# Attention with memories and a gated feed-forward in one kernel: the scores of a steady batch in one tiled excursion, output additions and stores issued later

## The chip, the cores and the metric

The kernel runs on 1 core of one Trainium2 chip. The metric is the device time of one execution in microseconds; three executions of the kernel before took 689.68, 690.58 and 690.91 us, median 690.58.

## The reference

`B, H, S, D, M = 8, 8, 576, 64, 32`; the model width is `H*D = 512`, the inner width 2048.

```python
a = softmax(phi, axis=2)                      # over the 576 tokens, per memory
k_m, v_m = a^T k, a^T v                       # 32 memories of 64 per head
attn = softmax(q k_m^T / 8, axis=-1)          # over the 32 memories
x = (attn v_m) of all heads side by side      # 4608 x 512
h = x @ w_in                                  # 4608 x 2048
g = h * clip(h + 3, 0, 6) / 6
out = g @ w_out                               # 4608 x 512, float32
```

## The kernel before

`attn v_m` and `x @ w_in` are not made one after the other. For each batch the memories' values are multiplied into `w_in` first (`fold`, L424, result `both`), so that the first product of the feed-forward is `both` times the 256 probabilities of a token (8 heads by 32 memories). The kernel rounds each float32 operand to a high and a low part, so that a product of two float32 matrices is three matmuls.

Batches 0 and 1 and the rounding of the weights run in an opening whose order is written out by hand. Batches 2 to 7 are **steady**. Each has 32 half-steps, numbered i = 0 to 31: 16 for the first 256 tokens (`half` 0), 16 for the other 320 (`half` 1). A unit is two half-steps (k = 0, 1) and makes two blocks of 128 of the inner width for a half of the tokens. In a half-step TensorE runs `gemm1` (6 matmuls into a PSUM bank `ph`, L712), ScalarE `relu` (L718), VectorE `gate` (L731, for the last 64 tokens L735). Each unit then feeds a seven-product scheme for the second matrix product: VectorE adds blocks (L741) and GpSimd two more (L745, L746), ScalarE rounds them (L752), VectorE takes the low parts (L757), and TensorE runs `products` (L680): 9 matmuls with kept weights in odd half-steps, 3 with kept and 9 with streamed weights in even ones, for the unit three half-steps back. The streamed weights (`stream`, three blocks of 256 KB for each unit) come from HBM through SyncE's queue, two units ahead.

A **turn** is where a half ends. Its sums leave PSUM through ScalarE (`leave_first`, L785, L786, L791) and VectorE (`leave_second`, L794, L795), GpSimd adds twice (`leave_third`, L799, L800) and SyncE stores 512 KB (L802). The additions are issued at the end of half-step 2 or 18, ahead of the next unit's own GpSimd work. In batches 2, 4 and 6 the first half-steps also run a rest stage for the last 64 tokens of two earlier batches.

The attention of the next batch (N) is laid between these half-steps by the tables `STEADY` and `EVERY`: "16 sc.N.0" puts a word into half-step 16. C is the current batch, M the one after next. In a half-step with k = 0 the words come behind the previous unit's rounding, with k = 1 ahead of the unit's own rounding, in both ahead of `products`. The words that matter here are `mem` (the memories' moments, L319), `sc` (scores, L357), `ct` (VectorE transposes the scores out of PSUM, L373), `cm` and `cs` (maximum, centring), `fo`, `vh`, `vl` (fold and its rounding, `vl` is L444), `bt` (transpose back, L403), `sp` (a broadcast load `nmxb` of row maxima, L284), `q` and `pt` (loads), `fetch` (weights for `fold`, L213).

Scores and folds use matmuls on a part of TensorE's array, 64 rows by 32 columns, eight places at once. Such a group between matmuls on the whole array is called an excursion here. Scores of a half go to two PSUM banks of 512 columns:

```python
self.psc = [psc[:, g, : W[hf]] for g in range(NG)]
```

## Time and profile before

| | |
|---|---|
| median of 3 runs | 690.58 us (689.68 to 690.91) |
| the profiled execution's own time | 689.36 us |
| its span, first to last instruction | 687.5 us |
| TensorE matmul busy | 670.7 us (98%) |
| TensorE weight loads busy | 580.2 us (84%) |
| VectorE busy | 573.2 us (83%) |
| ScalarE busy | 399.5 us (58%) |
| GpSimd busy | 338.1 us (49%) |
| mean of one L741, L745, L746 (groups of the page) | 522, 967, 465 ns |
| granted TensorE clock, mean | 0.996 |
| DMA | 163.95 MB, mean 238 GB/s |

Busy times of an engine are the union of its instructions. Matmuls overlap in the engine's pipeline, so a busy TensorE may still wait: the gaps are seen better between weight loads, which follow each other closely when nothing is late. Names such as `acc<-w,rounded` say what an instruction writes and reads.

### The profile page before, as it was taken

To read this page: it belongs to the slowest core of one execution; us is meant where nothing else is said; L and a number is where in the kernel's file an instruction comes from. 1 tells how busy PE (TensorE), PEld (TensorE's weight loads), DVE (VectorE), ACT (ScalarE), POOL (GpSimd) and SP (SyncE) were. 2 spreads that over 40 slices of the span, in tenths; PEclk is the share of its full clock that TensorE was granted. 3 is DMA by queue.
4 is the path that set the end of the run, shared out by engine and by line. 5 is a ranking of instruction groups with operands and counts; after the bars stand their busy time and mean duration, and the time that the engine had idled before them with its cause. 6 is when DMAs were issued, how large, how long until landed. Compare 5 with 4: busy or idle time off the path is not lost.

```text
span 687.5 us, 15317 instructions
## 1 busy us (share of the span) xinstructions
PE 670.7 (98%) x5810; PEld 580.2 (84%) x5814; DVE 573.2 (83%) x1062; ACT 399.5 (58%) x819; POOL 338.1 (49%) x354
## 2 busy tenths in 40 slices
PE   8999999899999999999999999999999999999997
PEld 4446778688879998899889998889889998899997
DVE  4899997898996769986898769986899778988765
ACT  4686796464654556564565645665465655665553
POOL 2644430788564436544556336543448245555433
PEclk9999999999999999999999999999999999999999
DMA  9998592454957978869584696869585593836351
GB/s 354 419 348 312 171 349 83 157 154 168 326 207 250 334 269 280 282 217 338 173 296 161 212 342 185 294 226 340 210 285 211 170 323 123 267 129 219 122 186 47
DMA packets 66817, 163.95 MB, mean 238 GB/s; under 512 B 7096, under 2 KB 12216, under 8 KB 64696
## 3 DMA queue, kind: packets, MB, share of 16 engines
q1 hardware_dynamic: 66664, 162.91, 67.6%
q8 instruction: 46, 0.75, 0.4%
q14 instruction: 27, 0.22, 0.1%
q10 hardware_dynamic: 80, 0.07, 0.0%
HBM read 140.92 MB, written 22.03 MB: 237 GB/s over the span
## 4 chain that ended last, share of the span: by engine, by line
PE 77%; DVE 11%; DMA 5%; ACT 4%; issue 2%; POOL 1%; SPq 0%; ACTq 0%; DVEq 0%; POOLq 0%
PE acc L680 38%; PE ph L712 20%; PE acc L541 6%; PE pv L424 4%; PE ph L487 4%; PE pk L319 2%; DMA qh<-in_qt 2%; DVE tmp L172 1%; DVE tmp L180 1%; DMA w<-w_kept 1%; DMA pnat<-in_pn 1%; DMA stream<-kept 1%; DVE tmp L175 1%; DVE gf L503 1%; PE psc L357 1%
## 5 line engine op out<-in xcount | busy, mean ns | idle before, releaser
L680 PE MATMUL acc<-w,rounded 128*128 128x256 f32 x1536 | 213.5, 280 | 2.2 <-DVE rounded L757 1.9
L680 PEld LDWEIGHTS acc<-w,rounded 128*128 128x128 f32 x1536 | 192.4, 188 | 26.7 <-ACT gf L718 8.5
L745 POOL TENSOR_TENSOR gated<-gated 128x256 f32<-128x256 f32 x96 | 92.8, 967 | 222.3 <-DVE gated L731 203.9
L712 PE MATMUL ph<-probs,both 128*128 128x256 f32 (+1 forms) x1152 | 180.7, 292 | 0.0
L757 DVE TENSOR_TENSOR rounded<-gated,rounded 128x384 fp32r<-128x384 f32 x192 | 147.8, 771 | 29.7 <-ACT rounded L752 28.8
L752 ACT CAST rounded<-gated 128x384 fp32r<-128x384 f32 x192 | 108.5, 567 | 92.9 <-DVE gated L741 85.0
L712 PEld LDWEIGHTS ph<-probs,both 128*128 128x128 f32 x1152 | 157.6, 188 | 1.0 <-issue 0.8
L718 ACT ACTIVATE gf<-ph,three 128x256 f32<-128x256 f32 (+1 forms) x192 | 95.9, 500 | 67.1 <-PE ph L712 64.8
L680 PE MATMUL acc<-stream,rounded 128*128 128x256 f32 x864 | 116.0, 277 | 0.6 <-DMA stream<-kept 0.5
L731 DVE SCALAR_TENSOR_TENSOR gated<-gf,ph 128x256 f32<-128x256 f32 x192 | 79.1, 412 | 35.9 <-ACT gf L718 35.3
L680 PEld LDWEIGHTS acc<-stream,rounded 128*128 128x128 f32 x864 | 105.9, 188 | 2.2 <-DMA stream<-kept 1.9
L541 PE MATMUL acc<-w,ghi 128*128 128x512 f32 x224 | 59.2, 397 | 0.0
L487 PEld LDWEIGHTS ph<-probs,both 128*128 128x128 f32 x336 | 48.6, 193 | 11.8 <-DVE gf L503 8.1
L487 PE MATMUL ph<-probs,both 128*128 128x320 f32 (+1 forms) x336 | 52.2, 304 | 4.4 <-DVE gf L503 3.9
L741 DVE TENSOR_TENSOR gated<-gated 128x256 f32<-128x256 f32 x96 | 50.1, 522 | 1.6
L541 PEld LDWEIGHTS acc<-w,ghi 128*128 128x128 f32 x224 | 40.4, 189 | 12.8 <-issue 4.4
L435 ACT CAST both<-pv 128x512 fp32r<-128x512 f32 x62 | 36.0, 584 | 18.6 <-PE pv L424 13.4
L746 POOL TENSOR_TENSOR gated<-gated 128x128 f32<-128x128 f32 x96 | 44.7, 465 | 0.0
L444 DVE TENSOR_TENSOR both<-pv,both 128x512 fp32r<-128x512 f32 x62 | 41.9, 677 | 2.5 <-ACT both L435 2.1
L190 POOL TENSOR_TENSOR w<-tmp,raw 128x512 uint32<-128x512 uint32 x12 | 19.3, 1629 | 44.7 <-DVE tmp L180 25.1
L497 ACT ACTIVATE gf<-ph,three 128x576 f32<-128x576 f32 (+2 forms) x36 | 24.6, 687 | 21.0 <-PE ph L487 15.0
L424 PE MATMUL pv<-w,kvT 64*32 64x512 f32 (+1 forms) x528 | 35.1, 588 | 1.6 <-DVE pnat L302 0.9
(116 smaller groups left out, 852.6 us busy)
## 6 DMA issues: line engine op xcount, KB each, us to landing
stream<-kept SPq DMA_DIRECT2D x222, 256.0 KB, 4.7
w<-w_kept SPq DMA_DIRECT2D x40, 512.0 KB, 6.9
kvt<-in_kv SPq DMA_DIRECT2D x32, 516.0 KB, 7.1
raw<-in_w SPq DMA_DIRECT2D x16, 512.0 KB, 7.8
raw<-in_w SPq DMA_DIRECT2D x8, 1024.0 KB, 12.4
out_t<-o SPq DMA_DIRECT2D x16, 512.0 KB, 3.2
kept<-stage SPq DMA_DIRECT2D x24, 256.0 KB, 2.8
pnat<-in_pn SPq DMA_DIRECT2D x8, 576.0 KB, 5.3
```

The lines of the kernel that those rows point to most:

```text
L424: nc.tensor.matmul(to[j * M : (j + 1) * M, g, k], self.kvT[rows, g, j * M : (j + 1) * M], chunk[rows, k, j].bitcast(F32), start=True, stop ...
L487: nc.tensor.matmul(dst, w[:, g, fs], x[:, g * n : (g + 1) * n], start=(i == 0), stop=(i == len(seq) - 1),)
L541: nc.tensor.matmul(accs[self.b, self.rest, k].rearrange("p (x c) -> p x c", c=VC), left[:, t * P : (t + 1) * P], w, start=k in self.first ...
L680: nc.tensor.matmul(dst, left[l], right[r], start=begin and n == 0, stop=end and n == 2, skip_group_check=True)
L712: nc.tensor.matmul(h, w[:, g, fs], x[:, g * self.n : (g + 1) * self.n], start=(i == 0), stop=(i == len(seq) - 1))
L718: nc.scalar.activation(self.gf, self.h[k], AF.Relu, bias=three)
L731: nc.vector.scalar_tensor_tensor(dst, by_tile(self.gf), 6.0, by_tile(self.h[k]), ALU.min, ALU.mult)
L741: nc.vector.tensor_tensor(g[:, 5:7], g[:, 7:9], g[:, 0:2], ALU.add)
L745: nc.gpsimd.tensor_tensor(g[:, 2:4], g[:, 0::8], g[:, 1:8:6], ALU.subtract)
L746: nc.gpsimd.tensor_tensor(g[:, 4], g[:, 1], g[:, 7], ALU.add)
L752: nc.scalar.copy(self.parts[0][:, at], self.g[:, 1:8][:, at])
L757: nc.vector.tensor_tensor(low[:, at], self.g[:, 1:8][:, at], high[:, at].bitcast(F32), ALU.subtract)
```

## The change

Three things change. First, the words `sc.N.0`, `ct.N.0`, `sc.N.1`, `ct.N.1` of half-steps 16 to 20 become `sb.N` (`both_scores`), all scores of both halves in one excursion in half-step 16, and `cp.N.2`, `cp.N.0`, `cp.N.1` (`pair_turn`), their transposes. 256 tokens of each half share the two banks of 512 columns. The last 64 tokens go into free columns of two banks in use: columns 320 to 383 of the `ph` bank that the next `gemm1` writes, and the first 64 columns of the bank in which the running half keeps one block of sums. `sb` and `cp.N.2` are played ahead of the rounding. Second, where no rest stage follows, `leave_third` is issued one half-step later, behind the unit's own GpSimd work, and the store one half-step later still, behind the fetch of streamed weights. Third, many other words of the tables move.

```diff
-0 kv.N.2 / 1 kv.N.4 / 2 kv.N.3 / 4 kv.N.0 / 6 kv.N.1
+0 kv.N.0 kv.N.2 / 4 kv.N.4 kv.N.3 kv.N.1
...
-q.N.1 mem.N / 12 nr.N nk.N / 13 fetch.N.1.1 / 15 tp.N pt.M tk.N / 16 sc.N.0 ct.N.0 / 18 kv.M.0 / 19 sc.N.1 / 20 ct.N.1
+nk.N pt.M fetch.N.0.1 q.N.0 / 15 tp.N fetch.N.1.1 tk.N / 16 sb.N cp.N.2 / 17 cp.N.0 / 19 kv.M.0 cp.N.1 / 20 cm.N.0 /
...
@@ -245,7 +245,7 @@
             heads += [qh[:, j] for j in range(n)]
         loaded.setdefault(b, {})["q", hf] = heads
 
-    vw, probs = {}, {}
+    vw, probs, sums, turn = {}, {}, {}, [0]
 
     class Attention:
 
@@ -371,6 +371,39 @@
                     nc.vector.transpose(st[:, g], self.psc[g])
             else:
                 nc.vector.transpose(st, self.psc_whole)
+
+        def both_scores(self):
+            pa = self.psum("psc")
+            m1, spare = sums[self.b - 1, 0][1], ph[1 - turn[0]]
+            heads = loaded[self.b]
+            ends = [spare[:, W[1] : W[1] + REST], m1[:, :REST]]
+            self.pairs = [(hf, 0, W[0], [pa[:, g, hf * W[0] : (hf + 1) * W[0]] for g in range(NG)]) for hf in range(2)]
+            self.whole = [pa[:, :, hf * W[0] : (hf + 1) * W[0]] for hf in range(2)]
+            self.pairs.append((1, W[0], REST, ends))
+            for k, (hf, at, n, to) in enumerate(self.pairs):
+                for j in range(NJ):
+                    for g in range(NG):
+                        rows = slice(g * D, (g + 1) * D)
+                        nc.tensor.matmul(
+                            to[g][j * M : (j + 1) * M],
+                            self.kvT[rows, g, j * M : (j + 1) * M],
+                            heads["q", hf][j][rows, at : at + n],
+                            start=k == 0 or k == 2 and g == 0,
+                            stop=True,
+                            tile_position=(g * D, j * M),
+                            skip_group_check=True,
+                        )
+
+        def pair_turn(self, k):
+            hf, at, n, to = self.pairs[k]
+            if hf not in self.st:
+                self.st[hf] = sb.tile([P, NG * W[hf]], F32, name="st", tag="st", bufs=3)
+            st = self.st[hf].rearrange("p (g s) -> p g s", g=NG)
+            if at == 0:
+                nc.vector.transpose(st[:, :, :n], self.whole[hf])
+                return
+            for g in range(NG):
+                nc.vector.transpose(st[:, g, at : at + n], to[g])
 
         def by_token(self, hf):
             return self.st[hf].rearrange("p (n m) -> p n m", m=M)
@@ -704,6 +737,7 @@
             f = 2 * self.u + k
             self.h = self.h if k else {}
             h = self.h[k] = ph[k][:, : self.n]
+            turn[0] = k
             both = vw[self.b, f * P // VC]
             fs = slice(f * P % VC, f * P % VC + P)
             phi, plo = probs[self.b, self.half]
@@ -798,13 +832,14 @@
             o, x = self.o, self.x
             nc.gpsimd.tensor_tensor(o[:, 1:3], x[:, 0:2], x[:, 2:4], ALU.add)
             nc.gpsimd.tensor_tensor(o[:, 0::3], o[:, 0::3], x[:, 1:3], ALU.add)
+
+        def store(self):
+            o = self.o
             row = self.b * S + OFF[self.half]
             nc.sync.dma_start(
                 out=out[row : row + 2 * P].rearrange("(i p) d -> p i d", i=2),
                 in_=o.rearrange("p (i x) c -> p i (x c)", i=2),
             )
-
-    sums = {}
 
     class RestUnit:
 
@@ -895,7 +930,7 @@
     ATTENTION = {
         "mx": A.maxima, "mt": A.maxima_turn, "mo": A.maxima_out, "sp": A.spread, "md": A.diagonal, "me": A.every, "xa": A.less_max,
         "xe": A.phi_exp, "kvm": A.memories, "nr": A.weights, "nk": A.normalise, "tp": A.turn, "tk": A.turned,
-        "sc": A.scores, "ct": A.scores_turn, "cm": lambda a, hf: a.reduce(hf, "mx"), "cs": A.centre,
+        "sb": A.both_scores, "cp": A.pair_turn, "sc": A.scores, "ct": A.scores_turn, "cm": lambda a, hf: a.reduce(hf, "mx"), "cs": A.centre,
         "csv": lambda a, hf: a.centre(hf, nc.vector), "dmv": lambda a, hf: a.divide(hf, nc.vector),
         "blv": lambda a, hf: a.back_low(hf, nc.vector),
         "ex": A.exponent, "ds": lambda a, hf: a.reduce(hf, "sm"), "dr": A.invert, "dm": A.divide, "bt": A.back,
@@ -978,10 +1013,12 @@
             ahead = unit.u + (-2 if unit.half else 2)
             if part == 1 and 0 <= ahead < NFT // 2:
                 fetch_streams(ahead)
+            if part == 1 and len(owed) == 1:
+                owed.pop()()
             if unit.last:
                 (unit.leave_second if part else unit.leave_first)()
                 if part and not between:
-                    unit.leave_third()
+                    owed[:] = unit.leave_third, unit.store
             return unit
 
         def finish_unit(unit, part):
@@ -998,6 +1035,7 @@
                 unit.products()
             us[-1].leave()
 
+        owed = []
         total_steps = 2 * len(units)
         for s in range(total_steps + LAG + 1):
             b, i = FIRST + s // 32, s % 32
@@ -1013,13 +1051,19 @@
                 unit.gemm1(k)
                 unit.relu(k)
                 unit.gate(k)
+                words = [] if resting else rows.get(i, [])
+                soon = [w for w in words if w.startswith("sb") or w.startswith("cp") and w.endswith(".2")]
+                for w in soon:
+                    play([w])
                 if k:
                     unit.sum_first()
                     unit.sum_second()
+                    if owed and len(owed) == 2:
+                        owed.pop(0)()
                 elif s >= 2 and not (resting and i == 2):
                     finish_unit(units[s // 2 - 1], 1)
-                if not resting:
-                    for w in rows.get(i, ()):
+                for w in words:
+                    if w not in soon:
                         play(group(w))
                 if k and not resting:
                     finish_unit(unit, 0)
@@ -1029,7 +1073,7 @@
                 us[i].prepare()
             unit = half_step(s - LAG - 1, (lambda: (us[3].total(), us[3].prepare())) if resting and i == 2 else None)
             if resting and i == 2:
-                after = {2: [unit.leave_third]} if unit else {}
+                after = {2: [unit.leave_third, unit.store]} if unit else {}
                 if b < B:
                     first = units[s // 2 - 1]
                     for k in range(3):
```

TensorE in half-steps 16 to 20 of batch 3 (`psc`, `ph` and `acc` are PSUM banks, `w` kept and `stream` streamed weights). Before:

```order
L712 MATMUL ph_2143<-probs,both 128x320 x6
L357 MATMUL psc<-qh,kvT 32x256 x8
L680 MATMUL acc<-w_6_1564,rounded 128x256 x3
L680 MATMUL acc<-stream,rounded 128x256 x9
L712 MATMUL ph_2144<-probs,both 128x320 x6
L680 MATMUL acc<-w_7_1526,rounded 128x256 x9
L712 MATMUL ph_2143<-probs,both 128x320 x6
L680 MATMUL acc<-w_7_1526,rounded 128x256 x3
L680 MATMUL acc<-stream,rounded 128x256 x9
L712 MATMUL ph_2144<-probs,both 128x320 x6
L357 MATMUL psc<-qh,kvT 32x320 x8
L680 MATMUL acc<-w_7_1526,rounded 128x256 x9
```

And with the change:

```order
L746 MATMUL ph_2143<-probs,both 128x320 x6
L387 MATMUL psc<-qh,kvT 32x256 x16
L387 MATMUL ph_2144<-qh,kvT 32x64
L387 MATMUL acc<-qh,kvT 32x64
L387 MATMUL ph_2144<-qh,kvT 32x64
L387 MATMUL acc<-qh,kvT 32x64
L387 MATMUL ph_2144<-qh,kvT 32x64
L387 MATMUL acc<-qh,kvT 32x64
L387 MATMUL ph_2144<-qh,kvT 32x64
L387 MATMUL acc<-qh,kvT 32x64
L713 MATMUL acc<-w_6_1564,rounded 128x256 x3
L713 MATMUL acc<-stream,rounded 128x256 x9
```

The second score group of 8 matmuls is gone from between `gemm1` and the 9 products; the first one has 24 matmuls in place of 8, the last eight alternating between two banks.

GpSimd at the turn from batch 4 to batch 5 (`gated` rows are a unit's own additions, `o` rows the output additions). Before:

```order
L745 TENSOR_TENSOR gated<-gated 128x256
L746 TENSOR_TENSOR gated<-gated 128x128
L799 TENSOR_TENSOR o<-o 128x512
L800 TENSOR_TENSOR o<-o 128x2x256
L745 TENSOR_TENSOR gated<-gated 128x256
L746 TENSOR_TENSOR gated<-gated 128x128
```

With the change, from the same unit on:

```order
L779 TENSOR_TENSOR gated<-gated 128x256
L780 TENSOR_TENSOR gated<-gated 128x128
L779 TENSOR_TENSOR gated<-gated 128x256
L780 TENSOR_TENSOR gated<-gated 128x128
L833 TENSOR_TENSOR o<-o 128x512
L834 TENSOR_TENSOR o<-o 128x2x256
```

The output additions stand behind two rows of the next unit that stood behind them.

SyncE's queue at the same turn (`out_t` is the store, `nmxb` the broadcast load, `kept` the streamed weights). Before:

```order
L234 DMA kvt<-in_kl 128x516
L802 DMA out_t<-o 128x2x512
L284 DMA nmxb<-nmx_5650 128x256
L676 DMA stream<-kept_1_97 128x512
L676 DMA stream<-kept_2_98 128x512
L676 DMA stream<-kept_0_96 128x512
L213 DMA w_5975<-w_kept_82 128x1024
```

With the change:

```order
L284 DMA nmxb<-nmx_5753 128x256
L709 DMA stream<-kept_1_97 128x512
L709 DMA stream<-kept_2_98 128x512
L709 DMA stream<-kept_0_96 128x512
L839 DMA out_t<-o 128x2x512
L709 DMA stream<-kept_1_100 128x512
```

The store no longer stands ahead of the broadcast and of the next three streamed blocks. Further on in batch 5, the loads of queries (`qh`). Before:

```order
L244 DMA qh<-in_qt 128x1024
L676 DMA stream<-kept_1_106 128x512
L676 DMA stream<-kept_2_107 128x512
L676 DMA stream<-kept_0_105 128x512
L244 DMA qh<-in_qt 128x640 x2
L676 DMA stream<-kept_1_109 128x512
```

With the change:

```order
L244 DMA qh<-in_qt 128x640 x2
L228 DMA ptile<-in_pt 128x576 x2
L213 DMA w_6149<-w_kept_81 128x1024
L244 DMA qh<-in_qt 128x1024
L709 DMA stream<-kept_1_109 128x512
```

The queries of the first 256 tokens (128x1024) were the first of the loads there and are now the last, behind the other queries, `phi` (`ptile`) and weights of `fold`.

## Rows read from the trace of the kernel before

**Rows 1.** The page's chain that ended last, share of the span by engine.

```profile
PE 77%; DVE 11%; DMA 5%; ACT 4%; issue 2%; POOL 1%; SPq 0%; ACTq 0%; DVEq 0%; POOLq 0%
```

**Rows 2.** Groups by line and shape: busy us, mean ns | idle us before, releasers.

```profile
L680 PE MATMUL acc<-w,rounded 128*128 128x256 f32 x1536 | 213.5, 280 | 2.2 <-DVE rounded L757 1.9 <-DVE o L567 0.3
...
L680 PEld LDWEIGHTS acc<-stream,rounded 128*128 128x128 f32 x864 | 105.9, 188 | 2.2 <-DMA stream<-kept 1.9
...
L444 DVE TENSOR_TENSOR both<-pv,both 128x512 fp32r<-128x512 f32 x62 | 41.9, 677 | 2.5 <-ACT both L435 2.1
...
L799 POOL TENSOR_TENSOR o<-o 128x512 f32<-128x512 f32 x12 | 16.9, 1404 | 17.0 <-ACT o L791 17.0
...
L800 POOL TENSOR_TENSOR o<-o 128x512 f32<-128x512 f32 x12 | 16.0, 1336 | 2.0 <-DVE o L795 2.0
```

**Rows 3.** Weight loads around the first score excursion (start us, us, instruction, idle before).

```profile
247.69 0.89 PEld L712 LDWEIGHTS ph<-probs,both 128*128 128x128 f32 x6
248.78 0.18 PEld L357 LDWEIGHTS psc<-qh,kvT 64*32 64x32 f32 x16 [0.19 <-ACT rounded L752]
249.37 0.41 PEld L680 LDWEIGHTS acc<-w,rounded 128*128 128x128 f32 x3 [0.41 <-issue]
```

**Rows 4.** Weight loads around the second score excursion.

```profile
254.87 0.88 PEld L712 LDWEIGHTS ph<-probs,both 128*128 128x128 f32 x6
255.95 0.18 PEld L357 LDWEIGHTS psc<-qh,kvT 64*32 64x32 f32 x16 [0.19 <-issue]
256.65 0.54 PEld L680 LDWEIGHTS acc<-w,rounded 128*128 128x128 f32 x4 [0.52 <-ACT gf L718]
```

**Rows 5.** Timeline, all engines, where batch 4 turns into batch 5.

```profile
454.34 1.29 POOL L800 TENSOR_TENSOR o<-o 128x512 f32<-128x512 f32 x1 [0.16 <-DVE o L795]
...
454.63 1.29 DVE L741 TENSOR_TENSOR gated<-gated 128x256 f32<-128x256 f32 x1
...
456.49 0.86 DVE L757 TENSOR_TENSOR rounded<-gated,rounded 128x384 fp32r<-128x384 f32 x1 [0.58 <-ACT rounded L752]
...
457.40 0.89 PEld L680 LDWEIGHTS acc<-w,rounded 128*128 128x128 f32 x7 [0.56 <-DVE rounded L757]
```

**Rows 6.** Weight loads near the end of the program.

```profile
669.88 0.30 PEld L680 LDWEIGHTS acc<-w,rounded 128*128 128x128 f32 x2 [0.59 <-DVE rounded L757]
```

**Rows 7.** Timeline of a pair of half-steps away from any turn.

```profile
225.60 0.43 DVE L741 TENSOR_TENSOR gated<-gated 128x256 f32<-128x256 f32 x1
...
226.61 0.85 DVE L757 TENSOR_TENSOR rounded<-gated,rounded 128x384 fp32r<-128x384 f32 x1 [0.58 <-ACT rounded L752]
...
228.01 1.09 PEld L680 LDWEIGHTS acc<-w,rounded 128*128 128x128 f32 x9
...
229.39 0.43 DVE L741 TENSOR_TENSOR gated<-gated 128x256 f32<-128x256 f32 x1
```

**Rows 8.** SyncE's queue: what it waited for, us in total, times, longest.

```profile
SPq L802 <- POOL o L800: 123.0, 12, 11.6
```

**Rows 9.** SyncE's issue of the broadcast after the turn of rows 5.

```profile
456.15 0.41 SPq L284 DMA_DIRECT2D nmxb<-nmx  x1
```

**Rows 10.** Stretches of 1 us after that turn: engines' busy us, clock, DMA share, GB/s.

```profile
459.00:460.00 1.00, 1.00 (x11) 1.00 (x10) 0.42 (x2) 0.87 (x2) 1.00 (x2) 1.00 0.50 59
...
461.00:462.00 1.00, 1.00 (x12) 1.00 (x11) 1.00 (x2) 0.66 (x2) 0.00 (x0) 1.00 1.00 385
```

**Rows 11.** Weight loads in batch 3 that waited for streamed blocks.

```profile
305.86 0.41 PEld L680 LDWEIGHTS acc<-stream,rounded 128*128 128x128 f32 x3 [0.73 <-DMA stream<-kept]
```

**Rows 12.** The last half-step of batch 3, VectorE and TensorE.

```profile
362.91 0.76 DVE L757 TENSOR_TENSOR rounded<-gated,rounded 128x384 fp32r<-128x384 f32 x1
...
363.82 1.18 PE L680 MATMUL acc<-w,rounded 128*128 128x256 f32 x9
```

**Rows 13.** Moments' matmuls and score loads in batch 5.

```profile
469.27 2.35 PE L319 MATMUL pk<-kvt,pnat 128*32 128x129 f32 x80
...
481.40 0.18 PEld L357 LDWEIGHTS psc<-qh,kvT 64*32 64x32 f32 x16 [0.19 <-ACT rounded L752]
```

More of the change, by code (lines that the diff above doesn't have):

```diff
@@ L90 @@
 THIRD = """
-0 kv.N.2 / 1 kv.N.4 / 2 kv.N.3 / 4 kv.N.0 / 6 kv.N.1
+0 kv.N.0 kv.N.2 / 4 kv.N.4 kv.N.3 kv.N.1
 """
 STEADY = """
-1 fo.C.3 vh.C.3.0 vl.C.3.0 / 5 bh.C.1 / 7 vh.C.3.1 / 9 vl.C.3.1 / 12 bl.C.1
+1 fo.C.3 vh.C.3.0 / 4 vl.C.3.0 / 8 vh.C.3.1 / 9 bh.C.1 vl.C.3.1 / 14 bl.C.1
 """
 EVERY = """
-3 sp.N / 5 fetch.N.1.0 / 6 xa.N.0 / 7 xa.N.2 fetch.N.0.0 / 8 xa.N.1 xe.N.0 fetch.N.0.1 / 9 xe.N.2 xe.N.1 q.N.0 / 11
-q.N.1 mem.N / 12 nr.N nk.N / 13 fetch.N.1.1 / 15 tp.N pt.M tk.N / 16 sc.N.0 ct.N.0 / 18 kv.M.0 / 19 sc.N.1 / 20 ct.N.1
-cm.N.0 / 21 cs.N.0 cm.N.1 / 22 pn.M fo.N.0 vh.N.0.0 vl.N.0.0 / 23 mx.M.0 fetch.N.2.0 vh.N.0.1 kv.M.1 vl.N.0.1 ex.N.0
-cs.N.1 ds.N.0 fetch.N.2.1 / 25 ex.N.1 fo.N.1 vh.N.1.0 dr.N.0 vl.N.1.0 dm.N.0 mx.M.1 / 26 vh.N.1.1 vl.N.1.1 bt.N.0
-fetch.N.3.0 / 27 ds.N.1 dr.N.1 mt.M bh.N.0 mo.M / 28 fo.N.2 vh.N.2.0 vl.N.2.0 / 29 bl.N.0 vh.N.2.1 vl.N.2.1
-fetch.N.3.1 kv.M.2 / 30 dm.N.1 / 31 kv.M.3 bt.N.1 kv.M.4
+2 sp.N / 7 xa.N.0 / 8 xe.N.0 xa.N.2 fetch.N.1.0 / 9 xe.N.2 xa.N.1 xe.N.1 / 10 fetch.N.0.0 / 11 mem.N / 12 q.N.1 nr.N
+nk.N pt.M fetch.N.0.1 q.N.0 / 15 tp.N fetch.N.1.1 tk.N / 16 sb.N cp.N.2 / 17 cp.N.0 / 19 kv.M.0 cp.N.1 / 20 cm.N.0 /
+21 fo.N.0 cm.N.1 / 22 cs.N.0 / 23 mx.M.0 vh.N.0.0 kv.M.1 vh.N.0.1 fetch.N.2.0 ex.N.0 vl.N.0.0 vl.N.0.1 ds.N.0
+fetch.N.2.1 / 24 cs.N.1 mx.M.1 / 25 fo.N.1 vh.N.1.0 vl.N.1.0 dr.N.0 dm.N.0 / 26 fetch.N.3.0 vh.N.1.1 ex.N.1 pn.M
+vl.N.1.1 mt.M bt.N.0 / 27 ds.N.1 kv.M.2 / 28 fo.N.2 vh.N.2.0 dr.N.1 dm.N.1 bh.N.0 kv.M.3 vl.N.2.0 / 29 kv.M.4 mo.M
+fetch.N.3.1 bl.N.0 / 31 vh.N.2.1 bt.N.1 vl.N.2.1
 """
```

## The prediction

> **What bounds the kernel now.** I read the chain of work first: TensorE carries 77% of it, VectorE 11%, DMA 5% [rows 1]. The table above gives TensorE 98% busy, so the question is what its time is made of that is not streaming whole matmuls. Two kinds are left. One is the price of excursions: between the end of one run of weight loads and the start of the next there is a hole in which the array drains, runs the small matmuls and drains again. The other is waits. The groups by line show them: products with kept weights waited 1.9 us for VectorE's L757, and loads of streamed blocks 1.9 us for their DMA [rows 2]. Of TensorE's clock nothing is to be had: the mean granted is 0.996, nearly always the 2.4 GHz level.
>
> The waits for L757 are five, of 0.56 to 0.59 us each where one sees them, ahead of a weight load. Four are at turns, into batches 3, 5, 7 and in the middle of batch 7; [rows 5] show one. The fifth is at the end of the program [rows 6], where no unit follows to hide the chain; nothing in the change touches it. At the turns the reader is to see this: GpSimd's L800 starts at 454.34 and takes 1.29 us, VectorE's L741 starts at 454.63 and takes 1.29 us too, three times its 0.43 in a pair away from a turn [rows 5, 7]. It ends 0.29 us behind L800. L757 follows it by way of ScalarE, and TensorE's third load of a group stands until L757 is done.
>
> **Scores in one excursion.** Before, the first leaves a hole from 247.69 + 0.89 = 248.58 to 249.37, 0.79 us, and the second one from 254.87 + 0.88 = 255.75 to 256.65, 0.90 us [rows 3, 4]. They differ in 64 columns and 0.11 us, so a column costs 1.7 ns, 256 columns 0.44 us, and the fixed part is 0.35 us. All 576 columns in one hole are then 0.35 + 0.98 = 1.33 us in place of 1.69: 0.36 us saved in each of the five batches 3 to 7, 1.8 us. That is the upper end. Nothing in the trace has 24 small matmuls in one hole. Each runs as two passes, so there are 48 loads in place of 16 (0.18 us, [rows 3]); if none of the added 32 hid under the streams, they would cost 0.36 us and eat it all. So 0 to 1.8 us. The first 16 loads end at 248.96, 0.41 us before the hole does, so streams run on while nothing loads; I stand near the upper end, at **1.5 us**.
>
> The transposes hold the same columns in four pieces instead of two; I put nothing for the two additional short ones, since `cp.N.2` is ahead of L757 in a half-step whose PE work grows by more than they take, and TensorE writes the borrowed `ph` columns' bank only after the 12 products that follow the excursion (9 of them load in 1.09 us [rows 7]). If that cover is gone, `gemm1` of half-step 17 waits.
>
> **Output additions later.** At the four turns L741 no longer meets L800. Undisturbed it is 0.86 us shorter, and the stall of 0.56 is smaller than that; L757 would end at 457.35 - 0.86 = 456.49, the stalled load would be due at 457.40 - 0.56 = 456.84, with 0.35 us to spare. So all four go: 3 x 0.56 and once 0.59, **2.3 us** at most. What is late next is the following unit. Behind L741's unit GpSimd now runs its own L745 and L746, 0.97 + 0.47 us (their means in the table above), and then 1.40 + 1.34 [rows 2], in all 4.18 us from the start of L741, while the next L741 comes 229.39 - 225.60 = 3.79 us later [rows 7]: it is held by 0.39 us, and in the worst case by 0.86 as now. The spare there is that of an undisturbed pair: L757 ends at 227.46, the third load is at 228.01 + 0.23, 0.78 us. At the turns between batches one copy `vl` (L444, 0.68 us [rows 2]) moves from half-step 1 to 4, into the same queue: 0.39 + 0.68 - 0.78 = 0.29 us may come back at three of the four, at worst 0.76. I take 0.1 at each: 2.3 - 0.3 = **2.0 us**, bounds 0 and 2.3.
>
> The Trainium skill, SBUF — State Buffer, section "Who interferes with whom", says that a VectorE instruction with two SBUF inputs contends with a GpSimd instruction that reads SBUF, and that whoever comes first holds the shared ports to its end. The trace agrees for L741 under L800 [rows 5]. It speaks against this change too, since the same two additions then sit over the next unit's L757 and L741; read strictly it gives the rival "the stall moves" below.
>
> **Store later.** SyncE's queue stood 123.0 us behind L800, in 12 stores [rows 8]: behind a store that waits, everything waits. At the turn into batch 5 that holds the broadcast until 456.15 [rows 9], and it then goes out just ahead of three streamed blocks. In the stretch 459 to 460 the DMA is half busy and moves 59 GB/s, where 461 to 462 moves 385 [rows 10]: the broadcast is slow traffic. In batch 3 the streamed block behind it is 0.73 us late [rows 11]. With the change the broadcast is issued before the store and before the streams, when the queue is free. That wait should go and a smaller one like it in batch 5; others (batch 2, the rest stage) have other neighbours. Of the 1.9 us I take **1.0**, bounds 0 and 1.9.
>
> **The rest of the tables.** Words move across many half-steps, and each one ahead of L757 takes from its spare. The tightest that I find is the last half-step of batches 3 and 5: L757 ends at 363.67, the third product starts at 363.82 + 0.23, so 0.38 us of spare [rows 12], and now `vl.N.2.1` (0.68 us) stands ahead of it. Against that, GpSimd's division `dm.N.1` moves two half-steps earlier and no longer holds L741 there. Cost 0 to 0.3 us twice; I take 0.1 each, **-0.2 us**.
>
> **Sum.** 1.5 + 2.0 + 1.0 - 0.2 = 4.3 us. Against the profiled execution's own 689.36 us (span 687.5 and 1.86 around it) that is 685.1. That execution was 1.2 us under the median of the three runs, so against the median it is 690.58 - 4.3 = **686.3 us**. About 0.2%, 1.4 us, is what a measurement of this kernel can tell from no change.
>
> **Rivals.**
> *The stall moves.* The additions, now behind L746, hold L757 and L741 of the next unit for the whole of L800, and with `vl` the stall comes back at each turn, as large as it was. For it: the sum above leaves no spare at three turns. Against: the fourth turn (middle of batch 7) has no attention words at all. Time: 690.58 - 1.5 - 1.0 + 0.2 = 688.3 us; chance 0.2.
> *Little happens.* The excursion of 24 costs what two did, and the streamed blocks wait as before, since the loads are only reordered; only part of the turns is left. Time: 690.58 - 1 = 689.6, within 0.2%; chance 0.13.
> *Slower: the scores wait for their queries.* The queries of the first 256 tokens are now the last of six loads, 2 x 320 + 2 x 288 + 512 + 512 = 2240 KB, and the scores of all tokens need them at one place. The loads' buffers come free when the moments' matmuls are done, at 469.27 + 2.35 = 471.62; the scores start at 481.40 [rows 13], 9.8 us later. At 385 GB/s the 2240 KB take 5.8 us, so I expect them in time. But two fetches of streamed blocks (1536 KB) share the queue; with these it is 9.8 us, exactly the room. If it is 2 us more, each of five batches waits 2 us: 690.58 - 4.3 + 10 = 696 us. It decides from 0.9 us a batch. Chance 0.12.
>
> **How the numbers follow.** My forecast has 0.55 (with better outcomes, up to 1.8 + 2.3 + 1.9 = 6.0 us saved, 684.6, and a little more where a wait's restart goes with it). Faster by over 0.2%: 0.55 + 0.2 + a little of the third = 0.76; within: 0.12; slower: 0.12. The range reaches from 683.3 to 690.4: it takes in the best bounds, the moved stall and the unchanged case, and leaves out the late queries.
>
> **What would show it.** Right: one hole near 1.33 us in half-step 16 and none in 19; L741 at 0.43 at all turns, no load waiting for L757 except the last; the broadcast issued some 4 us before the turn's streams; fewer waits for streamed blocks. Wrong: a hole of 1.6 us or more; loads waiting for L757 two half-steps behind a turn or at the ends of batches 3 and 5; score loads that wait for the DMA of `qh`; `gemm1` waiting for the transposes.

## The result and the profile after

The changed kernel takes 683.45 us (median of 4 runs, 683.22 to 684.54); the kernel before took 690.75 us in the runs beside it (4 runs, 689.68 to 691.56). The ratio is 0.9898, 95% interval 0.9881 to 0.9916: 0.8 to 1.2% faster. 686.3 us was forecast, with a range of 683.3 to 690.4. The spans of the profiled executions are 687.5 and 681.4 us, so 6.1 us are to be found in the two traces.

Lines of the changed kernel have other numbers: L680 became L713 (products), L712 L746 (`gemm1`), L718 L752 (`relu`), L731 L765 (`gate`), L741 L775 and L757 L791 (VectorE's addition and low part), L745 and L746 L779 and L780, L799 and L800 L833 and L834 (GpSimd's output additions), L802 L839 (store), L444 L477 (`vl`), L424 L457 (fold). The scores are L387.

The groups that answer to [rows 2], columns as there:

```profile
L713 PE MATMUL acc<-w,rounded 128*128 128x256 f32 x1536 | 212.3, 280 | 1.8 <-DVE rounded L791 1.4 <-DVE o L600 0.3
...
L713 PEld LDWEIGHTS acc<-stream,rounded 128*128 128x128 f32 x864 | 105.2, 188 | 0.0
...
L834 POOL TENSOR_TENSOR o<-o 128x512 f32<-128x512 f32 x12 | 20.1, 1677 | 0.0
...
L833 POOL TENSOR_TENSOR o<-o 128x512 f32<-128x512 f32 x12 | 18.4, 1530 | 0.0
```

Two things stand there. Loads of streamed blocks no longer wait at all (2.2 us before). Products still wait for VectorE's low part, 1.4 us where it was 1.9: most of the stall at the turns is left.

**Scores.** The weight loads around the one excursion, in batch 5 (the loads of the two `ph` and `acc` ends left out):

```profile
475.68 0.89 PEld L746 LDWEIGHTS ph<-probs,both 128*128 128x128 f32 x6
476.76 0.61 PEld L387 LDWEIGHTS psc<-qh,kvT 64*32 64x32 f32 x32 [0.19 <-issue]
...
477.90 0.42 PEld L713 LDWEIGHTS acc<-w,rounded 128*128 128x128 f32 x3
```

The hole is 477.90 - (475.68 + 0.89) = 1.33 us, where two holes made 1.69 [rows 3, 4]: 0.36 us saved, as worked out. In batches 3, 4 and 6 it is the same to 0.01 us, in batch 2 it is 1.46 us (246.95 + 0.89 to 249.30). Five batches: 4 x 0.36 + 0.23 = 1.7 us.

**The turn into batch 5**, all engines, to be held against [rows 5]:

```profile
452.03 1.61 POOL L833 TENSOR_TENSOR o<-o 128x512 f32<-128x512 f32 x1
...
452.76 1.43 DVE L791 TENSOR_TENSOR rounded<-gated,rounded 128x512 fp32r<-128x512 f32 x1
453.60 1.74 POOL L834 TENSOR_TENSOR o<-o 128x512 f32<-128x512 f32 x1
454.11 0.68 DVE L477 TENSOR_TENSOR both<-pv,both 128x512 fp32r<-128x512 f32 x1
...
455.15 0.48 DVE L775 TENSOR_TENSOR gated<-gated 128x256 f32<-128x256 f32 x1
...
457.12 0.89 PEld L713 LDWEIGHTS acc<-w,rounded 128*128 128x128 f32 x7 [0.53 <-DVE rounded L791]
```

L775 is short again, but the load still waits 0.53 us, one unit later than before (0.56). Now it is the low part of the other four blocks, L791 on 512 columns, that meets the addition: it takes 1.43 us, where the next one takes 0.69 (457.33), and ends 0.55 us after L833 has ended. Then `vl` follows, 0.68 us. At the turn in the middle of batch 7, where there is no `vl`, the stall is 0.29 us instead of 0.59:

```profile
641.97 1.05 DVE L775 TENSOR_TENSOR gated<-gated 128x256 f32<-128x256 f32 x1
...
644.50 0.77 PEld L713 LDWEIGHTS acc<-w,rounded 128*128 128x128 f32 x6 [0.29 <-DVE rounded L791]
```

The other two turns between batches show 0.55 (301.17) and 0.53 us (612.62). All four together gain about 0.4 us (0.07 at three, 0.30 at the fourth), 0.5 with restarts.

**Loads.** The half-step of [rows 11], from its first `gemm1` matmul to that of the next half-step, before and with the change:

```profile
303.80 0.84 PE L712 MATMUL ph<-probs,both 128*128 128x256 f32 x6
...
306.93 0.52 PE L712 MATMUL ph<-probs,both 128*128 128x256 f32 x3
```

```profile
302.08 0.84 PE L746 MATMUL ph<-probs,both 128*128 128x256 f32 x6
...
304.12 0.50 PE L746 MATMUL ph<-probs,both 128*128 128x256 f32 x3
```

It took 3.13 us and takes 2.04. So a wait of 0.73 us [rows 11] and one of 0.20 behind it (306.47) made the half-step 1.09 us longer. Counted in this way, waits for streamed blocks cost 0.9 us in batch 2, 1.1 in batch 3, 0.9 in the rest stage of batch 4 and 0.6 in batch 5: 3.5 us, all gone. A fold's wait for its weights went too (its matmuls at 289.72 waited 0.59 us), and another one came (0.44 at 444.04). With 1.7 for the scores and 0.5 for the turns that makes 5.7 of the 6.1 us.

### The profile page after: what moved, and what is told of

The parts are those of the page before. It is cut to its first block, busy times and chain, and to the rows that moved or that the text cites. A ratio compares the mean times of both kernels' runs of the same rounds, so it can differ in the third digit from the quotient of the medians.

```text
span 681.4 us, 15523 instructions
## 1 busy us (share of the span) xinstructions
PE 664.0 (97%) x5890; PEld 579.3 (85%) x5894; DVE 571.1 (84%) x1072; ACT 396.9 (58%) x819; POOL 345.7 (51%) x354
## 4 chain that ended last, share of the span: by engine, by line
PE 74%; DVE 14%; ACT 4%; DMA 3%; issue 2%; POOL 1%; SPq 1%; ACTq 0%; DVEq 0%; POOLq 0%
PE acc L713 36%; PE ph L746 18%; PE acc L574 7%; PE ph L520 4%; PE pv L457 4%; DVE rounded L791 2%; PE pk L319 2%; DMA kvt<-in_kv 2%; DVE tmp L172 1%; PE acc L911 1%; DVE gated L765 1%; DMA w<-w_kept 1%; DVE tmp L180 1%; DVE glo L554 1%; DVE both L477 1%
## 5 line engine op out<-in xcount | busy, mean ns | idle before, releaser
L713 PE MATMUL acc<-w,rounded 128*128 128x256 f32 x1536 | 212.3, 280 | 1.8 <-DVE rounded L791 1.4
L713 PEld LDWEIGHTS acc<-w,rounded 128*128 128x128 f32 x1536 | 192.2, 188 | 22.0 <-ACT gf L752 12.5
L779 POOL TENSOR_TENSOR gated<-gated 128x256 f32<-128x256 f32 x96 | 93.1, 970 | 217.3 <-DVE gated L765 211.3
L791 DVE TENSOR_TENSOR rounded<-gated,rounded 128x384 fp32r<-128x384 f32 x192 | 158.3, 825 | 36.1 <-ACT rounded L786 35.4
L746 PE MATMUL ph<-probs,both 128*128 128x256 f32 (+1 forms) x1152 | 180.6, 292 | 0.0
L746 PEld LDWEIGHTS ph<-probs,both 128*128 128x128 f32 x1152 | 157.5, 188 | 1.0 <-issue 0.8
L752 ACT ACTIVATE gf<-ph,three 128x256 f32<-128x256 f32 (+1 forms) x192 | 96.0, 500 | 45.3 <-PE ph L746 43.5
L713 PE MATMUL acc<-stream,rounded 128*128 128x256 f32 x864 | 113.6, 276 | 0.0
L713 PEld LDWEIGHTS acc<-stream,rounded 128*128 128x128 f32 x864 | 105.2, 188 | 0.0
L765 DVE SCALAR_TENSOR_TENSOR gated<-gf,ph 128x256 f32<-128x256 f32 x192 | 79.1, 412 | 27.1 <-ACT gf L752 26.5
L780 POOL TENSOR_TENSOR gated<-gated 128x128 f32<-128x128 f32 x96 | 49.2, 512 | 0.0
L775 DVE TENSOR_TENSOR gated<-gated 128x256 f32<-128x256 f32 x96 | 42.3, 441 | 1.6
L477 DVE TENSOR_TENSOR both<-pv,both 128x512 fp32r<-128x512 f32 x62 | 41.3, 674 | 1.0 <-ACT both L468 0.7
L457 PE MATMUL pv<-w,kvT 64*32 64x512 f32 (+1 forms) x528 | 35.1, 588 | 1.6 <-DVE pnat L302 0.9
```

What stands on the lines that cost most here:

```text
L457: nc.tensor.matmul(to[j * M : (j + 1) * M, g, k], self.kvT[rows, g, j * M : (j + 1) * M], chunk[rows, k, j].bitcast(F32), start=True, stop ...
L477: nc.vector.tensor_tensor(both[:, 1], src, both[:, 0].bitcast(F32), ALU.subtract)
L713: nc.tensor.matmul(dst, left[l], right[r], start=begin and n == 0, stop=end and n == 2, skip_group_check=True)
L746: nc.tensor.matmul(h, w[:, g, fs], x[:, g * self.n : (g + 1) * self.n], start=(i == 0), stop=(i == len(seq) - 1))
L752: nc.scalar.activation(self.gf, self.h[k], AF.Relu, bias=three)
L765: nc.vector.scalar_tensor_tensor(dst, by_tile(self.gf), 6.0, by_tile(self.h[k]), ALU.min, ALU.mult)
```

## Experiments

Each was timed beside the kernel before, in three groups (medians of before 690.3, 689.42 and 690.27 us). "Stream" is the idle time ahead of the loads of streamed blocks, in the profiled execution.

| run | median us (runs) | ratio to before, 95% | stream |
|---|---|---|---|
| kernel before, first profile | 690.75 (4) | | 2.2 |
| the change | 683.45 (4) | 0.9898 (0.9881 to 0.9916) | 0.0 |
| e1 before, store later | 687.78 (6) | 0.9968 (0.9956 to 0.9980) | 0.9 |
| e4 before, loads of the new tables | 687.00 (5) | 0.9948 (0.9933 to 0.9964) | 0.1 |
| e12 before again | 690.74 (1) | | 3.4 |
| e2 before, additions and store later | 687.71 (8) | 0.9966 (0.9953 to 0.9979) | 1.0 |
| e3 before, one excursion | 689.51 (12) | 0.9995 (0.9981 to 1.0008) | 1.2 |
| e5 change, two excursions | 692.35 (5) | 1.0045 (1.0033 to 1.0058) | 0.3 |
| e6 change, additions early | 683.95 (5) | 0.9924 (0.9910 to 0.9937) | 0.0 |
| e7 change, additions and store early | 684.29 (5) | 0.9927 (0.9914 to 0.9939) | 0.3 |
| e8 change, `vl` at 9 | 685.00 (5) | 0.9929 (0.9917 to 0.9942) | 0.0 |
| e9 change, additions apart, `vl` at 8 | 693.99 (6) | 1.0052 (1.0037 to 1.0068) | 0.8 |
| e10 change, additions apart, `vl` at 4 | 689.96 (12) | 0.9999 (0.9982 to 1.0016) | 3.0 |
| e11 as e9, last fetch earlier | 696.27 (6) | 1.0100 (1.0081 to 1.0120) | 5.2 |

### What made the loads late

e1, the store alone (the additions stay at the turn):

```diff
                 if part and not between:
                     unit.leave_third()
+                    owed.append(unit.store)
...
+            if part == 1 and len(owed) == 1:
+                owed.pop()()
```

> The kernel before with one edit: the store is issued one unit later, behind the fetch of streamed blocks; the additions stay where they were. Theory S (the store in SyncE's queue made the loads late, as the prediction has it): the waits for streamed blocks at the turns into batches 3 and 5 (1.1 and 0.6 us with their restarts) go, those of batch 2 and of the rest stage of batch 4 stay, so 1 to 1.7 us faster, and 0.7 more if the fold's wait for its weights after the turn into batch 3 goes too. Theory L (the order of the loads in the tables did it): 0 to 0.3 us.

e4, the places of the loads alone, old scores, additions and store (shortened to some of the words moved):

```diff
-3 sp.N / 5 fetch.N.1.0 / 7 fetch.N.0.0 / 8 fetch.N.0.1 / 9 q.N.0 / 11 q.N.1 / 13 fetch.N.1.1
+2 sp.N / 8 fetch.N.1.0 / 10 fetch.N.0.0 / 12 q.N.1 pt.M fetch.N.0.1 q.N.0 / 15 fetch.N.1.1
...
-27 mt.M mo.M / 29 fetch.N.3.1 kv.M.2 / 31 kv.M.3 kv.M.4
+26 fetch.N.3.0 pn.M mt.M / 27 kv.M.2 / 28 kv.M.3 / 29 kv.M.4 mo.M fetch.N.3.1
```

> The kernel before with the loads alone (keys and values, queries, phi, weights for the fold, row maxima out and back) at the half-steps of the changed kernel's tables; scores, additions and store as before. Theory L: the waits of batch 2 (0.9 us), of the rest stage of batch 4 (0.9 us) and of the fold after the turn into batch 3 (0.7 us) go, and with nmxb ahead of the store those of batches 3 and 5 (1.1 and 0.6) at least halve: 2.5 to 4 us faster. Theory S: what stands behind the store is late as before, 0.9 us or less. Rival: such waits are chance and differ between executions; then neither this nor the run with the store alone differs from the kernel before by what the traces say.

e12, the kernel before, unchanged:

> The kernel before once more, for a second profile. Theory (the loads' waits are chance as to place, the tables set how likely they are): the stalls for L757 at the four turns and the holes of the scores come back to within 0.03 us, the waits for loads stand elsewhere or have other sizes, by 1 us or more in sum. Rival: the same waits of 0.9, 1.1, 0.9, 0.6 and 0.7 us at the same half-steps.

The store alone is 1.4 to 3.0 us faster, the loads alone 2.5 to 4.6 us. So both theories are right, and each was wrong in ruling the other out. They don't add: with the new places of the loads, the store at the turn (e7, 684.29 us) and the store later (e6, 683.95 us) can't be told apart. SyncE's waits for GpSimd ahead of the store (us in total, times, longest) and the loads of streamed blocks in e7 show why:

```profile
SPq L839 <- POOL o L834: 133.2, 12, 12.5
...
L713 PEld LDWEIGHTS acc<-stream,rounded 128*128 128x128 f32 x864 | 105.4, 188 | 0.3 <-DMA stream<-kept 0.2
```

The queue stands behind the store for 133.2 us, as long as before (123.0, [rows 8]), and next to nothing is late. What differs is what is issued ahead of the streamed blocks when the queue is free again. Before, from 297.36 on, that was the store, the broadcast, three blocks and a fetch of 512 KB, with two more such fetches (303.34) behind the next three blocks:

```profile
297.36 0.40 SPq L802 DMA_DIRECT2D out_t<-o  x1
297.85 0.41 SPq L284 DMA_DIRECT2D nmxb<-nmx  x1
298.37 1.74 SPq L676 DMA_DIRECT2D stream<-kept  x3
300.16 0.48 SPq L213 DMA_DIRECT2D w<-w_kept  x1
```

In e4 six blocks follow the store, and the first fetch comes after them:

```profile
296.11 0.39 SPq L802 DMA_DIRECT2D out_t<-o  x1
296.60 6.13 SPq L676 DMA_DIRECT2D stream<-kept  x6
302.77 0.43 SPq L213 DMA_DIRECT2D w<-w_kept  x1
```

The second profile of before (e12) shows that such waits are partly chance. What doesn't depend on loads comes back, the stalls for L757 at the four turns within 0.04 us (0.56, 0.52, 0.56 and 0.59), the holes of the scores within 0.01. The waits for loads differ. The group of streamed loads, and loads of half-step 8 of batch 3 and of the rest stage of batch 6:

```profile
L680 PEld LDWEIGHTS acc<-stream,rounded 128*128 128x128 f32 x864 | 106.4, 188 | 3.4 <-DMA stream<-kept 3.1
...
305.90 0.41 PEld L680 LDWEIGHTS acc<-stream,rounded 128*128 128x128 f32 x3 [1.14 <-DMA stream<-kept]
...
524.41 0.98 PEld L680 LDWEIGHTS acc<-stream,rounded 128*128 128x128 f32 x6 [0.27 <-DMA stream<-kept]
```

The wait of batch 3 is there again, 1.14 us instead of 0.73; batch 6 has one that the first profile lacks; the fold's wait for its weights is missing. My reading is that the order of the loads sets how little margin there is, and each execution draws from it. Times don't prove it: the 4 runs of before beside the change spread over 1.9 us, the 4 of the change over 1.3. Of the two profiles of before the prediction read the one with fewer waits.

### What stalls at a turn

e2, additions and store later with the old tables:

```diff
                 if part and not between:
-                    unit.leave_third()
+                    owed[:] = unit.leave_third, unit.store
...
                     unit.sum_second()
+                    if owed and len(owed) == 2:
+                        owed.pop(0)()
```

> The kernel before with additions and store later, tables as they were. Stall theory (the additions of GpSimd hold VectorE for as long wherever they stand): L757 is late again one unit behind the turn in batches 3, 5 and 7 only if the copy vl stands in the same unit; here it stands at half-step 1, so each of the three stalls of 0.56 us should shrink to about 0.2 or go, and the fourth (middle of batch 7, 0.59) to about 0.25 as in the changed kernel: 1 to 2 us faster than the run with the store alone. Rival (the stall merely moves, whole): no difference to the run with the store alone.

687.71 us, against 687.78 for the store alone: the later additions are worth nothing here, which is the rival's time. At the three turns between batches the stall is 0.50 to 0.53 us; in the middle of batch 7 it shrinks to 0.29, as in the changed kernel, but two stalls of 0.33 us that e1 doesn't have stand further on (306.08 and 463.58). The unit behind the turn into batch 5 shows that `vl`, which stands at half-step 1 in e2, isn't needed for the stall. The second addition holds L741 just as well:

```profile
455.92 1.74 POOL L800 TENSOR_TENSOR o<-o 128x512 f32<-128x512 f32 x1
...
456.87 1.07 DVE L741 TENSOR_TENSOR gated<-gated 128x256 f32<-128x256 f32 x1
...
459.43 0.88 PEld L680 LDWEIGHTS acc<-w,rounded 128*128 128x128 f32 x7 [0.50 <-DVE rounded L757]
```

e6 and e7 take the changed kernel and put first the additions, then the store too, back to the turn:

```diff
                 if part and not between:
-                    owed[:] = unit.leave_third, unit.store
+                    unit.leave_third()
+                    owed[:] = [unit.store]
```

> The changed kernel with GpSimd's output additions at the turn again, the store still later. Stall theory: the stall is the same 0.6 us as with the additions later (at three turns it only moved), so within 0.3 us at those three, and 0.2 to 0.4 us slower at the turn in the middle of batch 7: 0 to 0.7 us slower in all. Rival (the later additions were worth the 2.0 us of the prediction): 2 us slower.

> The changed kernel with additions and store at the turn again. Theory S: the waits for streamed blocks behind the turns into batches 3 and 5 come back, 1 us or more slower than the run with the additions alone at the turn. Theory L (the order of the loads in the tables gives the room): within 0.3 us of that run.

Theory S for e7, 1 us or more behind e6, isn't borne out: it is 0.3. In e6 the three stalls at turns between batches are back at their old place with 0.56 us, and the fourth with 0.59:

```profile
453.39 0.89 PEld L713 LDWEIGHTS acc<-w,rounded 128*128 128x128 f32 x7 [0.56 <-DVE rounded L791]
```

How much the later additions are worth, the times leave open. The medians, 683.95 and 684.29 us, lie 0.5 and 0.8 us above the change, but in a group whose kernel before was 1.3 us faster; by the ratios it is 1.8 and 2.0 us, with intervals that just overlap. The traces speak for the stall theory: the four stalls sum to 2.27 us in e6 and to 1.90 in the change, and the spans of the two profiled executions differ by 0.5 us (681.9 and 681.4). In that difference there is also a wait that the change doesn't have, for the queries of batch 2's scores:

```profile
PE psc L387 <- DMA qh<-in_qt: 0.7, 1, 0.7
```

e8, `vl` out of the unit in which the additions now lie:

```diff
-1 fo.C.3 vh.C.3.0 / 4 vl.C.3.0 / 8 vh.C.3.1 / 9 bh.C.1 vl.C.3.1
+1 fo.C.3 vh.C.3.0 / 8 vh.C.3.1 / 9 bh.C.1 vl.C.3.0 vl.C.3.1
```

> The changed kernel with one word moved: the copy vl.C.3.0 (0.68 us of VectorE) from half-step 4 to 9, out of the unit on which the additions now lie. Theory: at the turns into batches 3, 5 and 7 the load that waits for L791 has 0.63 us of stall made of 0.74 us that GpSimd's addition holds L791 and 0.68 us of vl, less a spare of about 0.8; without vl the stall is at most that of the middle of batch 7 (0.39 us), or gone: 0.8 to 1.9 us faster than the changed kernel. Rival (the hold of the additions alone makes the stall): no faster.

It isn't faster (685.00 us, 1.6 above the change and, in its own group, 1.0 above e6), and the theory of e8 falls: the stall is still there. VectorE and TensorE at the turn into batch 5:

```profile
453.40 1.43 DVE L791 TENSOR_TENSOR rounded<-gated,rounded 128x512 fp32r<-128x512 f32 x1
...
455.20 1.07 DVE L775 TENSOR_TENSOR gated<-gated 128x256 f32<-128x256 f32 x1
...
457.76 0.89 PEld L713 LDWEIGHTS acc<-w,rounded 128*128 128x128 f32 x7 [0.53 <-DVE rounded L791]
```

With `vl` away, L775 comes early enough to meet L834, and waits for it: 1.07 us in place of the 0.48 that it took behind `vl`. So there may be two causes, each enough. e9 and e10 test that: the second addition goes three units later (and the store behind it), with `vl` at 8 or left at 4.

```diff
-owed[:] = unit.leave_third, unit.store
+owed[:] = unit.leave_third, None, None, unit.leave_fourth, unit.store
```

> The changed kernel with two edits: GpSimd's second output addition three units after the first (half-steps 9 and 25 in place of 3 and 19), and the copy vl.C.3.0 at half-step 8 in place of 4. Theory (two causes, each enough): L791 is late by 0.74 us behind the first addition, and then by either vl (0.68) or the second addition (0.64 on L775), against a spare of about 0.78; with both away all four stalls (3 x 0.63 and 0.39 us) go: 2.3 us faster than the changed kernel. Rival (the first addition's hold alone makes the stall): the stalls stay, within 0.3 us.

> The changed kernel with the second addition three units later, vl left at half-step 4. Theory of two causes: the stall at the turns into batches 3, 5 and 7 stays at about 0.6 us (vl alone makes it), the one in the middle of batch 7, where there is no vl, goes: 0.4 us faster than the changed kernel. Rival (the second addition is the cause): all four go, 2.3 us.

As to the stalls both come out as the theory of two causes has it. In e9 the same place shows one hold, of L791, then an undisturbed L775, and loads that don't wait, nor do they at the other three turns; in e10 (`vl` back) L775 is undisturbed as well, but late, and the load waits, as at the other two turns between batches (0.49 us each), while the stall in the middle of batch 7 is gone. First e9, then e10:

```profile
458.31 1.43 DVE L791 TENSOR_TENSOR rounded<-gated,rounded 128x512 fp32r<-128x512 f32 x1
...
460.11 0.43 DVE L775 TENSOR_TENSOR gated<-gated 128x256 f32<-128x256 f32 x1
...
461.11 0.85 DVE L791 TENSOR_TENSOR rounded<-gated,rounded 128x384 fp32r<-128x384 f32 x1 [0.58 <-PE acc L713]
461.84 0.30 PEld L713 LDWEIGHTS acc<-w,rounded 128*128 128x128 f32 x2
```

```profile
459.36 0.68 DVE L477 TENSOR_TENSOR both<-pv,both 128x512 fp32r<-128x512 f32 x1
...
460.39 0.42 DVE L775 TENSOR_TENSOR gated<-gated 128x256 f32<-128x256 f32 x1
...
462.30 0.77 PEld L713 LDWEIGHTS acc<-w,rounded 128*128 128x128 f32 x6 [0.48 <-DVE rounded L791]
```

In time both miss their expectation, by far: their medians are 10.5 and 6.5 us above the change's, in another group of runs, and neither is faster than before. The store moved with the second addition, to half-steps 10 and 26, and there it holds the loads of the next batch: it waits for the second addition, which ends at 471.17, and the queries go out 1.9 us behind the start of the moments' matmuls (469.78), where in the change it is 0.7. SyncE's queue in e10 and the score loads behind it:

```profile
471.20 0.39 SPq L842 DMA_DIRECT2D out_t<-o  x1
471.68 1.24 SPq L244 DMA_DIRECT2D qh<-in_qt  x2
473.01 1.41 SPq L228 DMA_DIRECT2D ptile<-in_pt  x2
474.47 0.43 SPq L213 DMA_DIRECT2D w<-w_kept  x1
475.00 0.38 SPq L244 DMA_DIRECT2D qh<-in_qt  x1
...
482.66 0.65 PEld L387 LDWEIGHTS psc<-qh,kvT 64*32 64x32 f32 x32 [0.94 <-issue]
...
PE psc L387 <- DMA qh<-in_qt: 1.9, 2, 1.2
```

The last row is from the list of waits: the scores waited 1.9 us in two batches for the queries. That is the rival "the scores wait for their queries", by its own mechanism, in a kernel in which the last query is issued at 475.00 and needed at 480.83 + 0.89 + 0.19 = 481.91 (end of the loads of `gemm1`, and the 0.19 us that the change idles there), 6.9 us later. In the change it was issued at 467.96 and needed at 476.76, 8.8 us later, and nothing waited. The streamed blocks wait as well in e10 (3.0 us in the table), and in e9 the later `vl` pushes the moments' inputs back, so that TensorE waits 0.50 us at 309.59 and, for ScalarE's `pnat`, 0.44 us at 311.91; each of batches 2 to 6 has such a pair, of 0.35 us or more, and e10, where only `vl` differs, has none. e9 also waits for L791 at places other than the turns, 0.30 and 0.29 us at the ends of batches 3 and 5 and 0.51 us in batch 7 (628.50). The single waits were not added up to the whole of the loss. Not tried: the additions apart with the store at its place of the change, which they rule out as they stand, since the store needs both.

e11, as e9, with `fetch.N.3.1` at half-step 27:

```diff
-27 ds.N.1 kv.M.2 / ... / 29 kv.M.4 mo.M fetch.N.3.1 bl.N.0
+27 ds.N.1 fetch.N.3.1 kv.M.2 / ... / 29 kv.M.4 mo.M bl.N.0
```

> As the run with the split additions and vl at half-step 8, and the fold's last load of weights (fetch.N.3.1) at half-step 27 in place of 29, ahead of keys, values and row maxima. Theory: the fold's wait for its weights behind a turn (0.5 us in the changed kernel's profile) can't occur, so no wait for a DMA at half-step 1, and 0 to 0.6 us faster than that run. Rival: streamed blocks behind the earlier load become late instead, 0.3 to 1 us slower.

The fold's wait is gone, as expected (0.6 us in e9), but the rival is right, and more: 2.3 us slower than e9. The streamed blocks wait 5.2 us in all. One of these waits is in the first half-step of batch 3:

```profile
288.18 0.42 PEld L713 LDWEIGHTS acc<-stream,rounded 128*128 128x128 f32 x3 [0.99 <-DMA stream<-kept]
```

Here the earlier load was paid for by the blocks behind it.

### What the excursion is worth alone

e3 puts it into the kernel before, e5 takes it out of the change:

```diff
-16 sc.N.0 ct.N.0 / 18 kv.M.0 / 19 sc.N.1 / 20 ct.N.1 cm.N.0
+16 sb.N cp.N.2 / 17 cp.N.0 / 18 kv.M.0 / 19 cp.N.1 / 20 cm.N.0
```

```diff
-16 sb.N cp.N.2 / 17 cp.N.0 / 19 kv.M.0 cp.N.1 / 20 cm.N.0
+16 sc.N.0 ct.N.0 / 19 kv.M.0 sc.N.1 / 20 ct.N.1 cm.N.0
```

> The kernel before with the scores of both halves in one excursion (and the transposes that belong to it) and nothing else. Theory: 0.36 us in each of five batches, 1.8 us faster; two half-steps (16 and 19) together 0.37 us shorter. Rival: additional loads of weights or a late transpose take half or more of it: 0.9 us or less.

> The changed kernel with the scores in two excursions again (half-steps 16 and 19). Theory: the excursion's 0.36 us in five batches come back, 1.8 us slower than the changed kernel. Rival: the merged excursion is worth half or less: 0.9 us slower or less.

Both theories miss, in the same way: the excursion doesn't come alone. For e3 the number of the rival holds (0.9 us or less), for e5 neither does. In e3 the hole is 1.33 us in all five batches, so 1.8 us are gained; but a new stall of 0.59 us stands in half-step 21 of each of them, 3.0 us without restarts. In batch 2:

```profile
258.00 1.29 POOL L834 TENSOR_TENSOR o<-o 128x512 f32<-128x512 f32 x1 [0.25 <-DVE o L829]
258.30 1.27 DVE L775 TENSOR_TENSOR gated<-gated 128x256 f32<-128x256 f32 x1
...
259.50 0.70 DVE L403 STREAM_TRANSPOSE st<-psc 128x512 f32<-128x512 f32 x1
...
261.06 0.65 PEld L713 LDWEIGHTS acc<-w,rounded 128*128 128x128 f32 x5 [0.59 <-DVE rounded L791]
```

It is the pattern of the turns once more: an addition that holds L775, and one more VectorE instruction (the transposes `cp.N.1`) ahead of L791. Why the old tables had room there with two excursions, and the new ones with one, was not tried apart; the new ones put the fold's excursion (half-step 21 in place of 22) ahead of the load that waits. In e5 it is the fold `fo.N.0`, at half-step 21 in the new tables and 22 in the old, that waits: it writes the PSUM banks that `ct.N.1` is still reading. Its waits, five of them, and the one of batch 3:

```profile
PE pv L457 <- DVE st L373: 7.1, 5, 1.4
...
336.26 0.18 PEld L457 LDWEIGHTS pv<-w,kvT 64*32 64x32 f32 x16 [1.68 <-DVE st L373]
```

In e5 the two holes are back (0.79 and 0.89 us in four of the five batches), but its 8.9 us over the change are mostly these waits (5 x 1.68 = 8.4 us ahead of the loads). So the hole costs what was worked out, wherever it was tried; in time no run shows it alone, and it needs the other words of the table to move with it.

## Why the prediction came out as it did

The time lies in the range, 0.15 us from its lower end, and that is in good part luck. The best bounds of the terms make 684.6 us; the end at 683.3 allowed another 1.3 us for restarts. 4.3 us were forecast where 6.1 are found between the two profiles, and the terms are not those of the sum: the loads brought more than was taken, the output additions less.

**Scores in one excursion: right.** 1.5 us taken, 1.7 found in the holes; the hole of 1.33 us is the forecast one. The additional loads hide (of 48, the first 32 take 0.61 us, inside the hole). The transposes cost nothing in the changed table, as reckoned; e3 shows that this is the table's merit.

**Output additions later: wrong.** 2.0 us taken, 0.4 to 0.5 found in the traces. The step that failed is "So all four go". It counted what the additions do to the next L741, 0.39 us, against a spare of 0.78, and left out what stands between: the low part on 512 columns, which the first addition makes 0.74 us longer (1.43 against 0.69). The additions also took 1.61 and 1.74 us where 1.40 and 1.34 were reckoned. After that the spare is used up, and either `vl` or the second addition makes the stall. The rival "the stall moves" was right at three of the four turns, also in its reservation on the middle of batch 7; its time, 688.3 us, was not, since the loads gave more than the 1.0 us that it took for them. The rule of the Trainium skill that the prediction cited there (SBUF — State Buffer, "Who interferes with whom") was, read strictly, the better forecast: L833 made L791 1.43 us long, and in the middle of batch 7 L834 made L775 1.05 us long.

**Store later: right in kind, too small, and not alone.** 1.0 us taken. The store alone brought 2.5 us (1.4 to 3.0, e1); store and tables together took away 3.5 us of waits for streamed blocks. The step mis-sized is "Of the 1.9 us I take 1.0, bounds 0 and 1.9". A wait lengthens its half-step by more than the idle time in front of the load (1.09 us for 0.73 and 0.20), and the places of the loads in the tables, which the sum didn't price at all, are by themselves worth as much as the store or more (e1, e4).

**The rest of the tables: -0.2 us taken.** No load waits at the ends of batches 3 and 5 in the change (the nine loads at 360.47 and at 516.47 follow without a gap), so this cost is nil. What the rest of the tables does is above: it makes room for the loads and for the transposes.

**Against the medians** the gain is 690.75 - 683.45 = 7.3 us, more than between the profiles. The profiled execution of before was 1.4 us under that median, and at least part of it is waits: the second profile has 3.4 us of idle time ahead of streamed blocks where the first had 2.2.

**Slower, the scores wait for their queries:** no such wait shows in the change, but one does in e10, where the last queries had 6.9 us to arrive instead of 8.8, and a single one of 0.7 us in e6, whose tables are those of the change. So the room is small, though the prediction counted it from the wrong point: it let the six loads begin when the moments' matmuls are done. In the change the first one goes out at 465.34, while these run (464.63 to 466.98), 11.4 us ahead of the scores where 9.8 were reckoned.

## What to carry to other kernels

When a stall is moved, price every instruction between its new place and the one that waits, not only the one that was late before; a hold that meets two instructions in turn may be enough twice over, and then taking away one cause shows nothing until the other is gone too. Where waits for loads are spread thinly over a profile, they were a lack of margin in one queue here: their sum differs between executions, idle time ahead of the load understates it, and what cures it is the order and the distance of all loads in that queue. A change to a table is one change: an excursion whose hole is 0.36 us shorter in each batch gave no gain clear of noise in the old table.

## What the hardware showed that was not expected

The hold works in both directions. GpSimd's two output additions took 1404 and 1336 ns on average at the turn [rows 2], and 1530 and 1677 ns behind the unit's own work: L834 starts at 453.60 there, while L791 runs to 454.19, and takes 1.74 us. Not every VectorE instruction is held: `vl` reads one operand from PSUM, and it ran beside L834 in its usual 0.68 us (454.11), while L791 and L775, with both operands in SBUF, waited. The same section of the Trainium skill's page SBUF — State Buffer says so for instructions with at most one SBUF input, and the trace agrees.
